# Attention and squared-ReLU feed-forward on one core: a last add in its own buffer, a later copy on GpSimd, and another rule for VectorE's hold-ups

## The chip, the cores and the metric

The kernel runs on one core of a Trainium2 chip. The metric is the device time of one execution in microseconds; before the change it is 402.41 us, the median of three runs (402.33 to 403.97). A core has TensorE (PE, matmuls; PEld, its weight loads), VectorE (DVE), ScalarE (ACT), GpSimd (POOL) and SyncE (SP), which only issues DMAs. Each engine executes its own queue in order, and engines wait for each other by semaphores.

## The reference

Eight sequences of 384 tokens go through grouped-query attention (16 query heads on 4 key and value heads, width 64), and the 1024 features of each token then through a feed-forward layer of width 2048 with a squared ReLU:

```python
scores = scale * np.matmul(q, k.transpose(0, 1, 3, 2))
scores = scores - np.max(scores, axis=-1, keepdims=True)
attn = np.exp(scores)
attn = attn / (np.sum(attn, axis=-1, keepdims=True) + 1e-09)
x = np.matmul(attn, v)              # then (8 * 384, 1024)
h = np.maximum(x @ w_in, 0.0)
out = h * h @ w_out                 # (3072, 1024), float32
```

## The kernel before, in words

**Batches and stages.** The work is done batch by batch (`b` from 0 to 7, one sequence each). A batch has scores (TensorE, L448), exponentials (ScalarE, L458), the product with the values (TensorE, L515 or L474) with its division (VectorE, L528 and L530), a transpose into `xT`, an up stage (`x @ w_in`), squares, and a down stage (`h*h @ w_out`). Attention of the next batches is interleaved with the feed-forward of the present one.

**Strassen's scheme.** From batch 2 on both products of the feed-forward are done with seven block products for eight, in float16. In the up stage (`strassen`, matmuls at L902) VectorE or ScalarE copies a product out of PSUM into `hr` (L878, L881), VectorE adds a later product to it (L886), ScalarE or GpSimd scales and clips it (L788, L791), and `close_squares` squares it into `h2T` on ScalarE, GpSimd or VectorE (L796, L800). In the down stage (`products`, `pair_of`, matmuls at L944) blocks of 128 tokens are taken in pairs: pair A holds the first two blocks of a batch; the third block of an even batch is kept in `h2x` (copied by GpSimd, L1199, in `sum_ops`) and makes pair D with the third of the next, odd batch. The left-hand sums of blocks are made by VectorE and GpSimd (L1180), those for the up stage by VectorE in `sums` (L658, the last of them L661); `summed` holds the batches for which the latter are recorded.

**A pair's results.** `done` in `pair_of` is called for each of the seven products. Products 1, 5 and 6 are copied from PSUM to a buffer `y_sb` with the scale `gs` (`copied`, L1094 on ScalarE, L1095 on VectorE); product 6 is copied twice, as `a2` and `b2`, if the two blocks have different scales. Products 2, 7, 3 and 4 are added to such a buffer by VectorE (`added`, L1101). After product 7 GpSimd adds its buffer `a3` to `p5` (L1133); product 4 is then added in place to `a3`. `put` sends a finished buffer to the output with a DMA of SP (L1308). In the last pair of the last batch product 3 comes last, as two whole pieces of 384 and 128 columns (L999), and the 128 columns of product 5 are added to `b2` ahead.

**Weights.** w_out is scaled and converted to float16 in 16 pieces (`here2`, L1226, on VectorE or ScalarE), and combined in `less2` (L1231) and `apart2` (L1238). These wait in the list `w2_q`. Ranges are measured by reductions whose result is spread over the partitions with a small cast (`top_of`, L675).

**A planner sets the order.** While the program is built, `Recorder.add` keeps a clock for each engine, with a cost in us given for each instruction, and the loops at the end (with `upkeep`) choose by these clocks which instruction comes next on which engine. `port=True` marks an instruction of VectorE that cannot run beside one of GpSimd; for it `Recorder.add` makes the cost longer by the overlap with GpSimd's last four instructions. A changed cost changes the clocks, and with them the order of all that is planned after it. In `upkeep` a piece of `w2_q` goes to VectorE if its clock is at most `lead` ahead of TensorE's, to ScalarE if that is true of its own. `Recorder.add` leaves out the wait for an earlier instruction of the same engine that only read what is now written.

The lines that choose the engine of a piece of w_out:

```python
lead = {"scalar": 0.6 if ff["b"] == 1 else 0.1, "vector": ... 0.9 if ff["b"] == 1 else 0.1}
able = [x for x in ("vector", "scalar") if eng in (x, "any") and R.clock[x] <= now + lead[x]]
```

Of the kernel before, what the change touches and what calls it, by code (L numbers as in the profile page):

```python
# [8 lines left out]
class Recorder:  # L9
# [36 lines left out]
    def add(self, eng, fn, reads=(), writes=(), dma=None, cost=0.1, issue=0.1, shared=(), after=(), port=False):  # L46
        i = len(self.ops)
        deps = self.deps_of(reads, writes)
        raw = {self.writer[r] for r in reads if r in self.writer}
        for r in reads:  # L50
            self.readers.setdefault(r, []).append(i)
        for w in writes:
            self.writer[w] = i
            self.readers[w] = []
        need = set(after)
        for d in deps:
            o = self.ops[d]
            if o["dma"] is None and o["eng"] == eng and dma is None:
                if eng in self.IN_ORDER or d not in raw:
                    continue  # L60
            need.add(d)
        if dma is not None:
            if dma in self.dma_last:
                need.add(self.dma_last[dma])
            self.dma_last[dma] = i
        start = max([self.clock[eng]] + [self.ops[d]["end"] for d in need])
        if dma is not None:
            self.clock[eng] = start + issue
            if eng == "gpsimd":
                self.pool.append((start, start + 0.3 * issue))  # L70
            q = eng
            begin = max(self.ring.get(q, 0.0), start + issue + 0.8)
            if shared and begin > start + issue + 0.8:
                shared = (3.0, shared[1])
            if shared and self.ring.get("gpsimd", 0.0) > begin:
                self.ring["gpsimd"] += shared[1]
                for o in self.ops:
                    if o["eng"] == "gpsimd" and o["dma"] is not None and o["end"] > begin:
                        o["end"] += max(0.0, min(shared[1], o["end"] - 1.2 - begin))
                cost = shared[0]  # L80
            self.ring[q] = begin + cost
            end = begin + cost + (1.5 if begin > 30 else 1.2 if eng == "gpsimd" else 0.7)
        else:
            if eng == "gpsimd":
                self.pool.append((start, start + cost))
            elif port:
                cost += 1.0 * sum(max(0.0, min(z, start + cost) - max(a, start)) for a, z in self.pool[-4:])
            self.clock[eng] = start + cost
            end = start + cost + (0.2 if eng == "tensor" else 0.07)
        self.ops.append(dict(eng=eng, fn=fn, dma=dma, need=need, signal=False, start=start, end=end))  # L90
        return i
# [57 lines left out]
def bass_gqa_attention__then__ffn_squared_relu_kernel(  # L149
# [619 lines left out]
    def close_squares(which):  # L769

        for x in [x for x in open_squares if which(x)]:
            open_squares.remove(x)
            i, r, dst, keys, relu, b = x
            assert b < FAST or b in ranged
            val = hr[r]
            two = val.rearrange("p (f t) -> p f t", f=2)
            end = R.ops[i]["end"]
            act, dve, pool = [max(R.clock[e], end) for e in ("scalar", "vector", "gpsimd")]
            slack = 1.5 * (b >= FAST and keys[0][1:] not in LAST_SQUARES)
            plans = [(act + 0.45 * (1 + relu) + slack, "ss"), (max(act + 0.52 * relu, pool) + 0.77 + 0.2, "sg")]  # L780
            if relu:
                plans.append((pool + 2.2 + 0.6, "gg"))
            elif not ff["now"]:
                plans.append((dve + 0.95 + 0.4, "sv"))
            one, other = min(plans)[1]
            to, by = small(b)
            if relu and one == "s":
                R.add("scalar", lambda e, val=val, to=to: e.activation(val, val, AF.Relu, scale=to),  # L788
                      reads=[("hr", r)] + by, writes=[("hr", r)], cost=0.54 if by else 0.45)
            elif relu:  # L790
                R.add("gpsimd", lambda e, val=val, to=to: e.tensor_scalar(val, val, to, 0.0, ALU.mult, ALU.max),  # L791
                      reads=[("hr", r)] + by, writes=[("hr", r)], cost=1.42)
            for _, c, t in keys:
                wrote[c, t] = b
            if other == "s":
                R.add("scalar", lambda e, dst=dst, two=two: e.activation(dst, two, AF.Square),  # L796
                      reads=[("hr", r)], writes=keys, cost=0.45)
            else:
                eng = dict(g="gpsimd", v="vector")[other]
                n = R.add(eng, lambda e, dst=dst, two=two: e.tensor_tensor(dst, two, two, ALU.mult),  # L800
                          reads=[("hr", r)], writes=keys, cost=0.77 if other == "g" else 0.95, port=other == "v")
                if other == "v":
                    hr_read[r] = (n,)

# [249 lines left out]
    def pair_of(b, pair, one, two):  # L1054
# [28 lines left out]

        ys = {}
        g1, g2 = b_1 % 3, b_2 % 3

        def slot(name):
            ys[name] = y_slot(b)
# [15 lines left out]
        def put(who, x, name, c0=0, c1=512):  # L1104
            bb, i3 = who
            send(bb, i3, 512 * x + c0, 512 * x + c1, ys[name], c0)

        def done(prod, at, *cols):
            flags.add(("done", b, pair, prod))
            if prod == 1:  # L1110
                copied(at, "a1", g1)
            elif prod == 2:
                added(at, g1, "a1", "a1")
                put(one, 0, "a1")
            elif prod == 5:
                copied(at, "p5", g2)
                ys["bank"] = at
            elif prod == 6:
                eng = copied(at, "a2", g2)
                if g1 != g2:  # L1120
                    copied(at, "b2", g1, eng)
                else:
                    ys["b2"] = ys["a2"]
                if b == B - 1 and pair == "D":
                    added(ys["bank"], g1, "b2", "b2", TAIL, 512, (R.writer[("y", ys["p5"])],))
            elif prod == 7:
                if g1 == g2:
                    slot("a3")
                else:
                    ys["a3"] = ys["a2"]  # L1130
                added(at, g2, "a2", "a3")
                y, z = ys["a3"], ys["p5"]
                R.add("gpsimd", lambda e: e.tensor_tensor(y_sb[z], y_sb[z], y_sb[y], ALU.add),  # L1133
                      reads=[("y", y), ("y", z)], writes=[("y", z)], cost=1.28)
                put(two, 1, "p5")
            elif prod == 3:
                added(at, g1, "b2", "b2", *cols)
                put(one, 1, "b2", *cols)
            else:
                added(at, g2, "a3", "a3")  # L1140
                put(two, 0, "a3")

        def product(prod, at):
            (a, na), (w, nw) = left(prod), right(prod)
# [4 lines left out]
    d_q = []  # L1149

    def sum_ops(b, double):
# [33 lines left out]
        def all_wrote(cs, ts=(0, 1)):  # L1185
            return all(wrote.get((c, t)) == b for c in cs for t in ts)
# [5 lines left out]
        if double:  # L1192
            for n, prod in ((0, 5), (1, 6), (3, None), (2, 3)):
                reads, go = op("D", n, None)
                d_q.append((lambda prod=prod: prod is None or ("done", b, "A", prod) in flags, reads, go, True))
        elif b < B - 1:
            keys = [("h2T", c, 1) for c in range(NFC)] + [("DS", b, "A", n, x) for n in (2, 3) for x in range(2)]
            d_q.append((lambda: all_wrote(range(NFC), (1,)), keys, lambda: R.add(
                "gpsimd", lambda e: e.tensor_copy(h2x[:, :, :], h2_16[:, :, 256:384]), reads=keys,  # L1199
                writes=[("h2x", b), ("h2x", b - 2)] + X_OVER, cost=2.0), True))  # L1200

# [325 lines left out]
    def below():  # L1527
        return not ff["tiles"] and not ff["now"]
# [95 lines left out]
    def upkeep(now):  # L1624
# [66 lines left out]
            add_sums(b)  # L1691
        while w2_q and w2_q[0][0]() and R.when(reads=w2_q[0][1], eng="none") <= now:
            eng = w2_q[0][3]
            lead = {"scalar": 0.6 if ff["b"] == 1 else 0.1, "vector": 0.5 if ff["b"] == FAST and not below() else -9 if m_q or lazy else 0.6 if below() else 0.9 if ff["b"] == 1 else 0.1}
            able = [x for x in ("vector", "scalar") if eng in (x, "any") and R.clock[x] <= now + lead[x]]
            if not able:
                break
            w2_q.pop(0)[2](*(able[:1] if eng == "any" else ()))
# [271 lines left out]
```

## Time and profile before

| | us |
|---|---|
| median of three runs | 402.41 |
| the profiled execution | 402.27 |
| its span, first to last instruction | 400.3 |
| TensorE busy | 389.6 |
| VectorE busy | 315.4 |
| ScalarE busy | 266.7 |
| GpSimd busy | 148.4 |

The granted clock of TensorE is 1.00 in nearly all of the span. All times are in us from the start of the span unless marked ns. A row of the order of work has the start, the length, engine, line, operation, the buffers written and read, shapes and a count; in brackets stand the idle time of the engine ahead of it and what ended that. A row of the waits has who waited, for whom, the total, how often and the longest. A row of a group has count, busy time and the mean in ns, and then idle time by what ended it. A row of a line's instructions has the shortest, median and longest in ns. Matmuls of 64 rows run in pairs on the two halves of the array, and their ends are modelled, so they overlap in the rows.

### The profile page before, as it was taken

To read this page: it belongs to the slowest core of one execution; us is meant where nothing else is said; L and a number is where in the kernel's file an instruction comes from. 1 tells how busy PE (TensorE), PEld (TensorE's weight loads), DVE (VectorE), ACT (ScalarE), POOL (GpSimd) and SP (SyncE) were. 2 spreads that over 40 slices of the span, in tenths; PEclk is the share of its full clock that TensorE was granted. 3 is DMA by queue.
4 is the path that set the end of the run, shared out by engine and by line. 5 is a ranking of instruction groups with operands and counts; after the bars stand their busy time and mean duration, and the time that the engine had idled before them with its cause. 6 is when DMAs were issued, how large, how long until landed. Compare 5 with 4: busy or idle time off the path is not lost.

```text
span 400.3 us, 15645 instructions
## 1 busy us (share of the span) xinstructions
PE 389.6 (97%) x7022; PEld 300.2 (75%) x7022; DVE 315.4 (79%) x652; ACT 266.7 (67%) x390; POOL 148.4 (37%) x169
## 2 busy tenths in 40 slices
PE   9999999999999999999999999998999999999995
PEld 6565764555666897588977999698987899789653
DVE  3689879899898987987987788986885688856644
ACT  6948999596655897768675587877783297426510
POOL 8665510245001664355332343444301144126111
PEclk9999999999999999999999999999999999999999
DMA  9999999995329873398597816697622223120022
GB/s 174 189 199 182 207 185 190 208 165 80 43 75 189 133 86 60 76 179 91 99 120 161 162 23 92 81 149 109 70 60 93 92 44 25 48 80 4 28 81 104
DMA packets 95634, 44.39 MB, mean 111 GB/s; under 512 B 75984, under 2 KB 89552, under 8 KB 95568
## 3 DMA queue, kind: packets, MB, share of 16 engines
q0 software_dynamic: 36672, 17.44, 35.6%
q1 hardware_dynamic: 58224, 25.47, 31.9%
q8 instruction: 55, 0.90, 1.0%
q10 hardware_dynamic: 672, 0.49, 0.4%
q14 instruction: 11, 0.09, 0.1%
HBM read 35.65 MB, written 12.58 MB: 121 GB/s over the span
## 4 chain that ended last, share of the span: by engine, by line
PE 78%; DVE 7%; DMA 7%; issue 4%; POOL 3%; ACT 1%; POOLq 0%; ACTq 0%; DVEq 0%
PE ps L944 27%; PE ps L902 26%; PE ps L515 6%; PE ps L448 6%; PE ps L611 6%; DMA w_in_sb<-in_moe_w_in_dram 5%; PE ps L1276 5%; DMA wx<-in_k_dram 1%; PE ps L474 1%; DVE w_out_sb L1226 1%; POOL w_in_sb L320 1%; DVE hr L624 1%; DVE y_sb L1101 1%; DVE w_out_sb L1238 1%; ACT h2T L796 1%
## 5 line engine op out<-in xcount | busy, mean ns | idle before, releaser
L458 ACT ACTIVATE expT<-ps 128x1024 bf16<-128x1024 f32 (+1 forms) x124 | 120.8, 1015 | 25.3 <-PE ps L448 25.2
L944 PE MATMUL ps<-w_out_sb,h2T 64*128 64x512 f16 x528 | 97.8, 376 | 0.5 <-DVE y_sb L1101 0.5
L902 PE MATMUL ps<-xT,w_in_sb 64*128 64x192 f16 x1152 | 84.8, 243 | 0.3 <-DVE y_sb L1101 0.3
L902 PEld LDWEIGHTS ps<-xT,w_in_sb 64*128 64x128 f16 x1152 | 71.2, 94 | 3.5 <-DVE y_sb L1101 0.5
L800 POOL TENSOR_TENSOR h2T<-hr 128x384 f16<-128x384 f32 x54 | 44.6, 845 | 51.7 <-ACT hr L788 51.6
L944 PE MATMUL ps<-area,xT 64*128 64x512 f16 x288 | 55.8, 376 | 0.0
L944 PEld LDWEIGHTS ps<-w_out_sb,h2T 64*128 64x128 f16 (+1 forms) x528 | 41.1, 94 | 15.8 <-DVE y_sb L1101 0.6
L448 PE MATMUL ps<-qT,kT 64*128 64x256 bf16 (+2 forms) x336 | 51.4, 326 | 0.6 <-ACT expT L458 0.4
L902 PE MATMUL ps<-s_all,wx 64*128 64x192 f16 x768 | 51.9, 242 | 0.0
L788 ACT ACTIVATE hr<-hr,bits 128x384 f32<-128x384 f32 x71 | 41.9, 609 | 11.8 <-DVE hr L886 11.5
L886 DVE TENSOR_TENSOR hr<-ps,hr 128x384 f32<-128x384 f32 x72 | 39.2, 555 | 9.4 <-PE ps L902 6.2
L902 PEld LDWEIGHTS ps<-s_all,wx 64*128 64x128 f16 x768 | 44.4, 94 | 0.9
L515 PE MATMUL ps<-v_aug,expT 64*128 64x65 bf16 x1680 | 43.7, 190 | 1.2 <-issue 0.6
L611 PE MATMUL ps<-xT,w_in_sb 64*128 64x384 bf16 x448 | 42.1, 323 | 1.0 <-DVE hr L624 0.6
L1101 DVE SCALAR_TENSOR_TENSOR y_sb<-ps,bits,y_sb 128x512 f32<-128x512 f32 (+2 forms) x38 | 26.9, 724 | 19.9 <-PE ps L944 13.3
L515 PEld LDWEIGHTS ps<-v_aug,expT 64*128 64x128 bf16 x1680 | 39.3, 94 | 2.7 <-DVE o_sb L530 0.7
L944 PE MATMUL ps<-area,h2T 64*128 64x512 f16 x144 | 36.4, 376 | 0.0
L1094 ACT ACTIVATE y_sb<-ps,bits 128x512 f32<-128x512 f32 x20 | 13.6, 687 | 33.7 <-PE ps L944 33.6
L878 ACT COPY hr<-ps 128x384 f32<-128x384 f32 x34 | 16.2, 479 | 27.2 <-PE ps L902 26.6
L611 PEld LDWEIGHTS ps<-xT,w_in_sb 64*128 64x128 bf16 x448 | 22.0, 94 | 16.2 <-DVE hr L624 1.8
L902 PE MATMUL ps<-s_all,w_in_sb 64*128 64x192 f16 x384 | 32.8, 243 | 1.3 <-issue 1.3
L902 PE MATMUL ps<-xT,wx 64*128 64x192 f16 x384 | 33.2, 243 | 0.7 <-issue 0.6
(147 smaller groups left out, 748.6 us busy)
## 6 DMA issues: line engine op xcount, KB each, us to landing
out_dram<-y_sb SPq DMA_DIRECT2D x45, 256.0 KB, 2.4
w_in_sb<-in_moe_w_in_dram POOLq DMA_DIRECT2D x8, 512.0 KB, 15.1
w_out_sb<-in_moe_w_out_dram POOLq DMA_DIRECT2D x4, 1024.0 KB, 28.9
q_st<-in_q_dram POOLq DMA_DIRECT2D x19, 192.0 KB, 5.2
q_st<-in_q_dram POOLq DMA_DIRECT2D x4, 384.0 KB, 23.1
k_st<-in_k_dram POOLq DMA_DIRECT2D x6, 192.0 KB, 4.1
k_st<-in_v_dram POOLq DMA_DIRECT2D x5, 192.0 KB, 5.0
wx<-in_q_dram POOLq DMA_DIRECT2D x2, 384.0 KB, 8.4
```

The costliest lines, as they stand in the source:

```text
L448: mm = pe.matmul(ps[:, base + x, m * wide:(m + 1) * wide], kT[at(b)][64 * x:64 * x + 64, u, :], q_cols(b, u // NJ, x, c0, c0 + wide))
L458: R.add("scalar", lambda e: e.activation(dst, src, AF.Exp, scale=0.125), reads=keys, writes=[("expT", slot(b, u), t) for u, _, _ in pieces ...
L515: m = pe.matmul(ps[:, p[x], n * DP:n * DP + D + 1], w, v_aug[b % 2][r, g * NJ + j, 0:D + 1], start=(n + j + y == 0), stop=(n + j + y == 2 ...
L611: m = pe.matmul(bank(4 + xs[x])[:, 0:S], w_in_sb[r, kc, c * 128:(c + 1) * 128], xT[b % NXT][r, kc, :], start=(phase < 2 and kc == 0), stop ...
L788: R.add("scalar", lambda e, val=val, to=to: e.activation(val, val, AF.Relu, scale=to), reads=[("hr", r)] + by, writes=[("hr", r)], cost=0. ...
L800: n = R.add(eng, lambda e, dst=dst, two=two: e.tensor_tensor(dst, two, two, ALU.mult), reads=[("hr", r)], writes=keys, cost=0.77 if other ...
L878: R.add("scalar", lambda e: e.copy(hr[r][:, :], src), reads=[("bank", at)], writes=[("hr", r)], cost=0.45, after=hr_read.pop(r, ()))
L886: R.add("vector", lambda e: e.tensor_tensor(hr[r][:, :], src, hr[r][:, :], ALU.add), reads=[("bank", at), ("hr", r)], writes=[("hr", r)], ...
L902: return lambda pe: pe.matmul(bank(at)[:, f * h:f * h + h], w[r, kc, c:c + 128], m[r, kc, :], start=(prod in (1, 5, 2) and y + f + kc == 0 ...
L944: return lambda pe: pe.matmul(bank(p.at)[:, 0:512], p.a(k, r), p.w(k, r), start=start, stop=stop, skip_group_check=True)
L1101: R.add("vector", lambda e: e.scalar_tensor_tensor(y_sb[z][:, c0:c1], bank(at)[:, c0:c1], gs[g], y_sb[y][:, c0:c1], ALU.mult, ALU.add), re ...
L1276: m = pe.matmul(bank(i)[:, 0:n], h2T[:, c, i3 * 128:(i3 + 1) * 128], w_out_sb[:, c, c0:c1], start=(c == 0), stop=(c == NFC - 1))
```

## The change

1. In `Recorder.add`, the extra cost of a marked instruction of VectorE is no longer the overlap with GpSimd's last four instructions, but the whole time until the end of one of the last six that has begun and not ended when it starts.
2. Squares on GpSimd or VectorE wait for those earlier readers of the same part of `h2T` that run on their own engine.
3. In the last pair of the last batch, the two copies of product 6 are put on ScalarE, and product 4 is added from `a3` into a buffer `a4` of its own.
4. GpSimd's copy into `h2x` is recorded only when the sums of the next batch are.
5. The lead of VectorE for pieces of w_out in batch 1 is 0.5 for 0.9.

```diff
@@ Recorder.add
-                cost += 1.0 * sum(max(0.0, min(z, start + cost) - max(a, start)) for a, z in self.pool[-4:])
+                cost += max([0.0] + [z - start for a, z in self.pool[-6:] if a <= start < z])
@@ close_squares
-                          reads=[("hr", r)], writes=keys, cost=0.77 if other == "g" else 0.95, port=other == "v")
+                          reads=[("hr", r)], writes=keys, cost=0.77 if other == "g" else 0.95, port=other == "v",
+                          after=tuple(d for key in keys for d in R.readers.get(key, ()) if R.ops[d]["eng"] == eng))
@@ pair_of
+        last = b == B - 1 and pair == "D"
...
-                eng = copied(at, "a2", g2)
+                eng = copied(at, "a2", g2, "scalar" if last else None)
                 if g1 != g2:
                     copied(at, "b2", g1, eng)
...
-                added(at, g2, "a3", "a3")
-                put(two, 0, "a3")
+                ys["a4"] = slot("a4") if last else ys["a3"]
+                added(at, g2, "a3", "a4")
+                put(two, 0, "a4")
@@ sum_ops
-            d_q.append((lambda: all_wrote(range(NFC), (1,)), keys, lambda: R.add(
+            d_q.append((lambda: b + 1 in summed and all_wrote(range(NFC), (1,)), keys, lambda: R.add(
@@ upkeep
-            lead = {..., "vector": ... else 0.9 if ff["b"] == 1 else 0.1}
+            lead = {..., "vector": ... else 0.5 if ff["b"] == 1 else 0.1}
```

More of the change, by code (lines that the diff above doesn't have):

```diff
@@ L1123, in done @@
                     ys["b2"] = ys["a2"]
-                if b == B - 1 and pair == "D":
+                if last:
                     added(ys["bank"], g1, "b2", "b2", TAIL, 512, (R.writer[("y", ys["p5"])],))
@@ L1693, in upkeep @@
             eng = w2_q[0][3]
-            lead = {"scalar": 0.6 if ff["b"] == 1 else 0.1, "vector": 0.5 if ff["b"] == FAST and not below() else -9 if m_q or lazy else 0.6 if below() else 0.9 if ff["b"] == 1 else 0.1}
+            lead = {"scalar": 0.6 if ff["b"] == 1 else 0.1, "vector": 0.5 if ff["b"] == FAST and not below() else -9 if m_q or lazy else 0.6 if below() else 0.5 if ff["b"] == 1 else 0.1}
             able = [x for x in ("vector", "scalar") if eng in (x, "any") and R.clock[x] <= now + lead[x]]
```

## The prediction

> **What bounds the kernel now.** I read the page's busy table first, then who waited for whom on TensorE, then the busy time by stage, and last the order of work around the places that the edits touch.
>
> The page's first part, the waits of TensorE, and busy time of three stages (stretch, its length, then PE, PEld, DVE, ACT and POOL busy with instruction counts, clock, DMA share, GB/s):
>
> ```profile
> PE 389.6 (97%) x7022; PEld 300.2 (75%) x7022; DVE 315.4 (79%) x652; ACT 266.7 (67%) x390; POOL 148.4 (37%) x169
> ...
> PE ps L902 <- issue: 2.0, 2, 1.3
> PE ps L611 <- DVE hr L624: 0.6, 2, 0.4
> PE ps L515 <- DVE o_sb L530: 0.5, 1, 0.5
> PE ps L944 <- DVE y_sb L1101: 0.5, 1, 0.5
> PE ps L902 <- DVE y_sb L1101: 0.3, 1, 0.3
> ...
> 79.30:97.70 18.40, 17.76 (x218) 10.17 (x216) 17.52 (x34) 16.54 (x21) 9.92 (x11) 1.00 0.90 150
> 137.00:141.00 4.00, 3.46 (x98) 2.84 (x94) 3.97 (x8) 2.41 (x5) 1.56 (x2) 1.00 0.73 98
> 396.00:400.30 4.30, 0.05 (x1) 0.00 (x0) 1.63 (x3) 0.00 (x0) 0.00 (x0) 0.87 0.51 183
> ```
>
> TensorE is the bound: 389.6 of 400.3 us. Of the 10.7 us that it is not busy, 4.25 lie behind its last matmul (last row), and the waits for VectorE sum to 0.6 + 0.5 + 0.5 + 0.3 = 1.9 us. So an edit of other engines can win in two places only: the 4.25 us tail, and those 1.9 us. The 2.0 us named issue are waits that the trace gives no cause for; no edit aims at them.
>
> **The tail: a buffer of its own, copies on ScalarE.** VectorE, then GpSimd, TensorE and SP at the end; then VectorE's forms from 391 us; then an earlier add beside GpSimd:
>
> ```profile
> 392.07 1.41 DVE L1095 TENSOR_SCALAR y_sb<-ps,bits 128x512 f32<-128x512 f32 x2 [2.70 <-PE ps L944]
> 393.52 1.03 DVE L1101 SCALAR_TENSOR_TENSOR y_sb<-ps,bits,y_sb 128x128 f32<-128x128 f32 x2
> 396.00 1.73 DVE L1101 SCALAR_TENSOR_TENSOR y_sb<-ps,bits,y_sb 128x512 f32<-128x512 f32 x3 [1.45 <-POOL y_sb L1133]
> ...
> 394.63 1.27 POOL L1133 TENSOR_TENSOR y_sb<-y_sb 128x512 f32<-128x512 f32 x1 [10.82 <-DVE y_sb L1101]
> ...
> 394.13 1.92 PE L999 MATMUL ps<-w_out_sb,xT 128*128 128x384 f16 x16
> ...
> 395.92 2.64 SPq L1308 DMA_DIRECT2D out_dram<-y_sb  x4
> 397.76 0.81 SPq L1308 DMA_DIRECT2D out_dram<-y_sb  x2
> ...
> L1101 DVE SCALAR_TENSOR_TENSOR y_sb<-ps,bits,y_sb 128x512 f32<-128x512 f32 x2 | 1.5, 751 | 1.4 <-POOL y_sb L1133 1.4
> L1101 DVE SCALAR_TENSOR_TENSOR y_sb<-ps,bits,y_sb 128x128 f32<-128x128 f32 x2 | 0.7, 350 | 0.1
> L1101 DVE SCALAR_TENSOR_TENSOR y_sb<-ps,bits,y_sb 128x384 f32<-128x384 f32 x1 | 0.6, 609 | 0.0
> ...
> 382.55 1.26 POOL L1133 TENSOR_TENSOR y_sb<-y_sb 128x512 f32<-128x512 f32 x1 [10.96 <-DVE y_sb L1101]
> 383.44 0.75 DVE L1101 SCALAR_TENSOR_TENSOR y_sb<-ps,bits,y_sb 128x512 f32<-128x512 f32 x1 [0.98 <-PE ps L944]
> ```
>
> VectorE stands idle for 1.45 us at 394.55: product 4's add writes the buffer that GpSimd is still reading. With its own buffer it starts at 394.55 and takes 0.75. Product 3 then sets the pace: its first part, 384 of 512 columns of the 1.92 us from 394.13, is ready near 395.6 and takes 0.61, its second when TensorE ends at 396.05, and takes 0.35. VectorE ends near 396.65 instead of 397.73, 1.08 us earlier. The add may run beside GpSimd at full speed: the one at 383.44 began inside GpSimd's 382.55 to 383.81 and took 0.75 all the same.
>
> The end is the last store, though. SP issues four, the last two 0.81 / 2 = 0.4 us apart, the first when GpSimd is done at 395.92, which does not move. The four then go at 395.92, 396.3, 396.7 and 397.05; the last one is now at 398.2. By issue the gain is 1.1 us. By bandwidth (stretches behind the end; then the last store's time to landing):
>
> ```profile
> 396.60:399.60 3.00, 0.00 (x0) 0.00 (x0) 1.03 (x3) 0.00 (x0) 0.00 (x0) 0.93 0.74 262
> 397.75:398.25 0.50, 0.00 (x0) 0.00 (x0) 0.00 (x0) 0.00 (x0) 0.00 (x0) 1.00 1.02 385
> 398.25:398.75 0.50, 0.00 (x0) 0.00 (x0) 0.00 (x0) 0.00 (x0) 0.00 (x0) 1.00 0.44 157
> ...
> out_dram<-y_sb SPq DMA_DIRECT2D x1, 64.0 KB, 1.7
> ```
>
> the four stores move 3.0 x 262 = 786 KB; at the best rate shown, 385 GB/s, that takes 2.04 us instead of 3.0, a gain of 0.9. I take 0.9, since both must hold, with 0 (the add waits after all) and 1.1 as ends. The two copies cost nothing either way: on VectorE the pair takes 1.41 us, and ScalarE is free; what they feed (the 128-column add, and behind it L999) starts within 0.1 us of where it did. If ScalarE were late, L999 would be, one for one.
>
> **GpSimd's copy behind the next sums.** The stretch where this copy hurts, GpSimd, VectorE, TensorE, then the range of the cast, and where the sums end:
>
> ```profile
> 252.91 1.90 POOL L1199 COPY area<-h2T 128x2048 f16<-128x2048 f16 x1
> 253.07 1.83 DVE L675 CAST top_w<-bits 128x128 bf16<-128x128 f32 x1
> 254.82 0.74 DVE L1101 SCALAR_TENSOR_TENSOR y_sb<-ps,bits,y_sb 128x512 f32<-128x512 f32 x1
> 255.62 0.39 PE L944 MATMUL ps<-w_out_sb,h2T 64*128 64x512 f16 x1 [0.46 <-DVE y_sb L1101]
> ...
> L675 DVE CAST top_w<-bits x14: 226/227/1829, 57.6 to 346.6; 128x128 bf16<-128x128 f32 x14
> ...
> 259.09 0.20 DVE L661 TENSOR_SCALAR bits<-bits 128x1 f32<-128x1 f32 x1
> 261.43 1.27 POOL L1133 TENSOR_TENSOR y_sb<-y_sb 128x512 f32<-128x512 f32 x1 [1.34 <-DVE y_sb L1101]
> ```
>
> A cast of 0.23 us became 1.83 and ended when the copy did; the add behind it came late, and TensorE lost 0.46 us. With the copy behind L661, at 259.1 to 261.0, the cast is back at 0.23 and these 0.46 us go. What the copy meets there is the pair's add at 261.43, 0.4 us after it; should one of GpSimd's loads go ahead of the copy, that add is late, and with it product 4's add, which writes what GpSimd reads there. What such a late add costs TensorE is shown by the wait of L902 for L1101, 0.3 us. The copy also moves behind the loads of queries that it held back, which can only be early by that. I take -0.45, between -0.46 and +0.3. The two other copies count as zero: TensorE's waits in the list are not at them.
>
> **Hold-ups in full, a shorter lead, a wait of squares for their own engine.** In batch 1 VectorE is full (17.52 of 18.40 us above) and converts w_out between evictions:
>
> ```profile
> 88.80 4.37 DVE L1226 TENSOR_SCALAR w_out_sb<-w_out_sb,bits 128x1024 f16<-128x1024 bf16 x6
> 93.08 1.00 DVE L624 TENSOR_SCALAR hr<-ps 128x384 f32<-128x384 f32 x2
> 94.15 0.82 PE L611 MATMUL ps<-xT,w_in_sb 64*128 64x384 bf16 x8 [0.19 <-DVE hr L624]
> ...
> L1226 DVE TENSOR_SCALAR w_out_sb<-w_out_sb,bits x14: 472/482/1680, 82.2 to 94.0; 128x1024 f16<-128x1024 bf16 x14
> L1226 ACT ACTIVATE w_out_sb<-w_out_sb,bits x2: 1147/1150/1152, 79.3 to 84.3; 128x1024 f16<-128x1024 bf16 x2
> ```
>
> Six in a row hold up the eviction of hr. A lead of 0.5 for 0.9 lets about one fewer (0.48 us) stand ahead of it, which covers the two waits for L624 (0.6 us in all). The formula itself moves both ways: it charges more where GpSimd is already running, nothing where GpSimd begins later. It changes the order from 73 us on, and I cannot derive that order by hand. I take -0.3 for both together, half of the 0.6, with ends of -1.9 (all waits for VectorE go) and the loss of the third rival.
>
> The squares' waits (rows of GpSimd's idle time):
>
> ```profile
> POOL h2T L800 <- ACT hr L788: 51.6, 25, 5.9
> POOL ident L1333 <- POOL ident L1332: 0.2, 1, 0.2
> ...
> L800 POOL TENSOR_TENSOR h2T<-hr x54: 816/826/1263, 133.3 to 366.9; 128x384 f16<-128x384 f32 x54
> ```
>
> a wait of GpSimd for itself showed 0.2 us; at 54 squares at most 11 us, against 51.6 us that the same squares wait for ScalarE. It counts as nothing; without that cover, what is queued behind a square on GpSimd, the sums of squares and the loads, would be late, and TensorE one for one. VectorE's few squares get the same wait, for sums that it finished a batch before.
>
> GpSimd's squares reach 1263 ns beside 826, so a hold-up runs the other way too, which neither formula charges to GpSimd; that 0.44 us lies in its idle time as well.
>
> **Sum.** 402.27 (this execution: span 400.3 and 2.0 around it; the median 402.41 is 0.14 above) - 0.9 - 0.45 - 0.3 = 400.6.
>
> **Rivals.** (1) The order settles better everywhere: all 1.9 us of waits for VectorE go (0.45 of them the copy's). 402.27 - 0.9 - 1.9 = 399.5; the hidden lateness at 137 to 141 us, where 0.54 us of TensorE are idle, makes 399.0. For it: the casts and conversions that were held up are just those that the new formula sees. Against: most such GpSimd work was queued after VectorE's op, which no formula sees.
> (2) Only the tail comes, and the new order elsewhere gives its gain back: 402.27 - 0.9 + 0.2 = 401.6. For it: any reorder of a queue that is 95% full makes some eviction late.
> (3) Slower: with the shorter lead, conversions go to ScalarE at 1.15 us each. It has 18.40 - 16.54 = 1.86 us free in that stage, so from the second moved one each delays the exponentials that free TensorE's banks. Six moved make 6.9 - 1.86 = 5.0 us, less 1.35 elsewhere: 405.9. From three on it eats the gain; from five on the kernel is slower by 0.5%. Against: ScalarE takes one only when it is at most 0.6 us behind TensorE.
> (4) The add and GpSimd shut each other out. In its own buffer the add starts at 394.55, just before GpSimd's 394.63; if GpSimd had to wait for it, GpSimd would begin at 395.3, and the four stores would go 0.67 us later than above, the last at 397.7 for 398.2. The tail gives 0.4: 402.27 - 0.4 - 0.75 = 401.1. If the add waited instead, it would give nothing: 401.5. Against: the add at 383.44, though there GpSimd had begun first.
> The Trainium skill (SBUF — State Buffer, section "Who interferes with whom") has a rule that bears on this: a VectorE instruction with two inputs in SBUF contends with a GpSimd instruction that reads SBUF, one with at most one does not, and whoever issues first keeps the shared ports for its whole length. This add reads PSUM, one buffer and one factor per partition; if the factor counts as an input, the rule gives this rival's 401.1, if not, the forecast, and the 0.75 us at 383.44 agrees with the latter as far as one order of starts can.
>
> **Chances.** 0.5% of 402.41 is 2.0 us, about what a measurement of this kernel can tell from no change; faster is below 400.4, slower above 404.4. Forecast 0.47, half of whose own range of 399.7 to 401.5 lies a little over the border (0.20 faster, 0.27 same). Rival 1: 0.20, faster. Rival 2: 0.17, same. Rival 3: 0.11 (0.09 slower, 0.02 same). Rival 4: 0.05, same. That makes 0.40, 0.51 and 0.09. The range 398.7 to 402.7 holds the forecast and rivals 1, 2 and 4.
>
> **What would show it.** Right: no idle VectorE between the adds at 394 us, its last add within 0.7 us of TensorE's last matmul; every L675 below 1.3 us in batch 4; fewer than six L1226 in a row. Wrong: more than three L1226 on ScalarE, new waits of TensorE for expT, or issue waits that grew: they would outweigh the rest without any edit having aimed at them.

## The result, and the profile after

The changed kernel takes 400.76 us, the median of 13 runs (399.2 to 401.99), against 402.33 us for the kernel before, measured beside it (13 runs, 401.19 to 403.97). The ratio is 0.9957, with a 95% interval of 0.9938 to 0.9976: between 1.0 and 2.5 us faster. The profiled execution took 401.29 us, its span 399.2 us.

The page's first part of the changed kernel, and TensorE's waits between 70 and 392 us (who, for whom, total, times, longest). The inserted lines move later line numbers by one to three: L902, L944, L999, L1101, L1133, L1199 and L1226 of before are L903, L945, L1000, L1103, L1135, L1202 and L1229 here.

```profile
PE 388.7 (97%) x7019; PEld 298.7 (75%) x7022; DVE 312.0 (78%) x648; ACT 270.0 (68%) x395; POOL 145.7 (36%) x168
...
PE ps L903 <- issue: 3.5, 2, 2.1
PE ps L611 <- DVE hr L624: 1.0, 2, 0.7
PE ps L515 <- ACT expT L458: 0.4, 1, 0.4
PE ps L903 <- DVE y_sb L1103: 0.3, 1, 0.3
PE ps L945 <- DVE y_sb L1103: 0.3, 1, 0.3
```

TensorE's waits for other engines are not fewer: 2.0 us here, 1.9 before. Two of them went (the add behind the held cast, and `o_sb` at 140 us), those in batch 1 grew from 0.6 to 1.0 us, and two are new: one of 0.4 us for ScalarE's `expT` at 148 us, and one of 0.3 us for VectorE's add at 211 us (L945). The waits named issue grew from 2.6 us (2.0 and 0.6) to 3.5.

The end, in the order of work of the changed kernel, VectorE, ScalarE, GpSimd, TensorE and SP:

```profile
393.27 2.02 DVE L1103 SCALAR_TENSOR_TENSOR y_sb<-ps,bits,y_sb 128x128 f32<-128x128 f32 x3 [4.00 <-ACT y_sb L1096]
393.70 1.59 DVE L1103 SCALAR_TENSOR_TENSOR y_sb<-ps,bits,y_sb 128x512 f32<-128x512 f32 x2
395.54 1.07 DVE L1103 SCALAR_TENSOR_TENSOR y_sb<-ps,bits,y_sb 128x384 f32<-128x384 f32 x2 [0.25 <-PE ps L1000]
...
391.97 1.26 ACT L1096 ACTIVATE y_sb<-ps,bits 128x512 f32<-128x512 f32 x2 [1.04 <-PE ps L945]
...
394.53 1.27 POOL L1135 TENSOR_TENSOR y_sb<-y_sb 128x512 f32<-128x512 f32 x1 [10.83 <-DVE y_sb L1103]
...
394.03 1.92 PE L1000 MATMUL ps<-w_out_sb,xT 128*128 128x384 f16 x16
...
395.32 2.15 SPq L1311 DMA_DIRECT2D out_dram<-y_sb  x4
```

VectorE no longer idles for GpSimd: product 4's add is the second of the two at 393.70 and ends at 395.29, while GpSimd works from 394.53 to 395.80. The last add ends at 396.61, 0.66 us behind the last matmul (395.95), and the first of the last four stores goes at 395.32, 0.5 us ahead of GpSimd's end, not after it. From the last matmul to the end of the span it is 3.25 us now, for 4.21 (the 4.25 of the prediction counts to the end of its stretch, 400.30; the span ends at 400.26).

The casts, GpSimd's copy, and the stretches of the copy, of batch 1, of 137 us and of the larger issue wait (stretch, length, busy time of PE, PEld, DVE, ACT, POOL, clock, DMA share, GB/s):

```profile
L675 DVE CAST top_w<-bits x14: 226/227/228, 56.8 to 346.5; 128x128 bf16<-128x128 f32 x14
...
259.30 1.90 POOL L1202 COPY area<-h2T 128x2048 f16<-128x2048 f16 x1
261.15 1.28 POOL L1135 TENSOR_TENSOR y_sb<-y_sb 128x512 f32<-128x512 f32 x1
...
250.00:264.00 14.00, 14.00 (x215) 11.76 (x212) 11.28 (x27) 11.32 (x13) 6.88 (x7) 1.00 0.67 85
79.30:97.70 18.40, 17.45 (x218) 9.94 (x216) 18.11 (x37) 15.76 (x20) 11.06 (x12) 1.00 0.93 157
137.00:141.00 4.00, 4.00 (x118) 3.74 (x112) 3.82 (x8) 3.54 (x6) 1.17 (x3) 1.00 0.28 53
179.60:181.60 2.00, 0.59 (x16) 0.43 (x14) 0.66 (x2) 1.93 (x3) 1.49 (x2) 1.00 0.18 34
```

No cast is held any more, TensorE is busy throughout the copy's stretch and at 137 us, but in batch 1 it has 17.45 us instead of 17.76, and near 181 us it stands for 1.4 us without a cause in the trace.

### The profile page after: what moved, and what is told of

Read it like the earlier page. It is cut to its first block, busy times and chain, and to the rows that moved or that the text cites. A ratio compares the mean times of both kernels' runs of the same rounds, so it can differ in the third digit from the quotient of the medians.

```text
span 399.2 us, 15638 instructions
## 1 busy us (share of the span) xinstructions
PE 388.7 (97%) x7019; PEld 298.7 (75%) x7022; DVE 312.0 (78%) x648; ACT 270.0 (68%) x395; POOL 145.7 (36%) x168
## 4 chain that ended last, share of the span: by engine, by line
PE 91%; DVE 4%; ACT 2%; issue 1%; DVEq 0%
PE ps L945 31%; PE ps L903 28%; PE ps L448 7%; PE ps L611 7%; PE ps L515 7%; PE ps L1279 5%; ACT expT L458 2%; PE ps L474 2%; PE ps L574 1%; DVE hr L624 1%; DVE w_out_sb L1229 1%; PE ps L1366 1%; DVE y_sb L1103 1%; PE ps L549 1%; PE ps L1000 0%
## 5 line engine op out<-in xcount | busy, mean ns | idle before, releaser
L945 PE MATMUL ps<-w_out_sb,h2T 64*128 64x512 f16 x528 | 98.0, 376 | 0.0
L903 PE MATMUL ps<-xT,w_in_sb 64*128 64x192 f16 x1152 | 84.1, 243 | 0.5 <-DVE y_sb L1103 0.3
L903 PEld LDWEIGHTS ps<-xT,w_in_sb 64*128 64x128 f16 x1152 | 70.9, 94 | 3.7 <-PE ps L903 0.5
L800 POOL TENSOR_TENSOR h2T<-hr 128x384 f16<-128x384 f32 x52 | 42.0, 828 | 50.1 <-ACT hr L788 50.0
L945 PE MATMUL ps<-area,xT 64*128 64x512 f16 x288 | 55.7, 376 | 0.0
L903 PE MATMUL ps<-s_all,wx 64*128 64x192 f16 x768 | 51.6, 243 | 0.0
L945 PEld LDWEIGHTS ps<-w_out_sb,h2T 64*128 64x128 f16 (+1 forms) x528 | 39.2, 94 | 16.4 <-ACT h2T L796 0.3
L1103 DVE SCALAR_TENSOR_TENSOR y_sb<-ps,bits,y_sb 128x512 f32<-128x512 f32 (+2 forms) x38 | 27.1, 725 | 23.2 <-PE ps L945 12.4
L903 PEld LDWEIGHTS ps<-s_all,wx 64*128 64x128 f16 x768 | 44.2, 94 | 0.9
L515 PE MATMUL ps<-v_aug,expT 64*128 64x65 bf16 x1680 | 43.1, 190 | 0.5 <-ACT expT L458 0.4
L515 PEld LDWEIGHTS ps<-v_aug,expT 64*128 64x128 bf16 x1680 | 39.2, 94 | 1.9 <-ACT expT L458 0.8
L945 PE MATMUL ps<-area,h2T 64*128 64x512 f16 x144 | 35.9, 376 | 0.0
L903 PE MATMUL ps<-s_all,w_in_sb 64*128 64x192 f16 x384 | 32.4, 242 | 2.1 <-issue 2.1
L903 PE MATMUL ps<-xT,wx 64*128 64x192 f16 x384 | 32.9, 242 | 1.4 <-issue 1.4
L1135 POOL TENSOR_TENSOR y_sb<-y_sb 128x512 f32<-128x512 f32 x9 | 11.9, 1319 | 61.1 <-DVE y_sb L1103 61.1
```

What stands on the lines that cost most here:

```text
L515: m = pe.matmul(ps[:, p[x], n * DP:n * DP + D + 1], w, v_aug[b % 2][r, g * NJ + j, 0:D + 1], start=(n + j + y == 0), stop=(n + j + y == 2 ...
L903: return lambda pe: pe.matmul(bank(at)[:, f * h:f * h + h], w[r, kc, c:c + 128], m[r, kc, :], start=(prod in (1, 5, 2) and y + f + kc == 0 ...
L945: return lambda pe: pe.matmul(bank(p.at)[:, 0:512], p.a(k, r), p.w(k, r), start=start, stop=stop, skip_group_check=True)
L1103: R.add("vector", lambda e: e.scalar_tensor_tensor(y_sb[z][:, c0:c1], bank(at)[:, c0:c1], gs[g], y_sb[y][:, c0:c1], ALU.mult, ALU.add), re ...
```

## The experiments

Single executions of one kernel lie up to 5.5 us apart (the kernel before, 25 runs in one comparison: 400.64 to 406.18), so beside the medians each trace was cut at places that every order has: the first matmul of batch 0's down stage (53 us), the first matmul of the up stages of batches 2 to 7, the last matmul, and the end of the span. All lengths are in us; the last two columns are the sums of TensorE's waits from 70 to 392 us, named issue (with those that the trace puts on TensorE's own scores) and for other engines.

| kernel | to up 2 | up 2 to 3 | 3 to 4 | 4 to 5 | 5 to 6 | 6 to 7 | 7 to last matmul | to the end | issue | others |
|---|---|---|---|---|---|---|---|---|---|---|
| before | 73.9 | 41.9 | 52.9 | 39.7 | 52.7 | 37.1 | 44.6 | 4.21 | 2.6 | 1.9 |
| before2 | 74.1 | 42.0 | 52.3 | 39.7 | 52.4 | 37.1 | 44.6 | 4.21 | 1.6 | 1.9 |
| tail | 73.8 | 41.9 | 52.5 | 39.7 | 52.7 | 37.1 | 44.6 | 3.23 | 2.0 | 1.9 |
| a4 | 73.6 | 41.9 | 52.3 | 39.7 | 53.0 | 37.1 | 44.6 | 3.24 | 2.1 | 1.9 |
| copy | 73.6 | 42.0 | 52.5 | 39.0 | 53.3 | 37.1 | 44.6 | 4.22 | 2.9 | 1.4 |
| lead | 73.5 | 42.4 | 52.4 | 39.8 | 52.5 | 37.1 | 44.6 | 4.20 | 1.2 | 3.1 |
| formula | 74.0 | 41.2 | 53.0 | 39.5 | 51.3 | 37.1 | 44.6 | 4.21 | 0.4 | 2.2 |
| formtail | 74.0 | 41.2 | 53.6 | 39.5 | 51.1 | 37.1 | 44.6 | 3.24 | 1.0 | 2.2 |
| formtailcopy | 74.1 | 40.6 | 53.7 | 39.0 | 52.0 | 37.1 | 44.6 | 3.25 | 1.7 | 1.8 |
| notail | 74.6 | 40.8 | 54.5 | 39.0 | 51.6 | 37.1 | 44.6 | 4.21 | 2.4 | 1.9 |
| after | 74.4 | 40.8 | 53.8 | 39.0 | 53.5 | 37.1 | 44.6 | 3.25 | 3.5 | 2.0 |
| after2 | 74.6 | 40.8 | 54.5 | 39.0 | 52.3 | 37.1 | 44.6 | 3.25 | 3.1 | 1.9 |
| fewturns | 74.4 | 40.8 | 54.5 | 39.0 | 51.5 | 37.1 | 44.6 | 3.24 | 2.3 | 1.9 |
| fewloads | 74.6 | 40.8 | 51.9 | 39.0 | 51.1 | 37.1 | 44.6 | 3.28 | 0 | 1.9 |

Most columns repeat within 0.1 us for one order of work; the first differs by up to 0.5 us (73.6 to 74.1 in before's order). The stages from up 3 to 4 and from up 5 to 6 differ more, by up to 1.9 us between executions of one order, and in them the issue waits lie.

**The tail alone, and everything but the tail.** On the kernel before, and taken back from the changed one:

```diff
+        last = b == B - 1 and pair == "D"
-                eng = copied(at, "a2", g2)
+                eng = copied(at, "a2", g2, "scalar" if last else None)
-                added(at, g2, "a3", "a3")
-                put(two, 0, "a3")
+                ys["a4"] = slot("a4") if last else ys["a3"]
+                added(at, g2, "a3", "a4")
+                put(two, 0, "a4")
```

> The kernel before with the third edit alone: product 4 of the last pair into a buffer of its own, product 6's two copies on ScalarE. The order of everything ahead of the last pair is unchanged. My theory: the whole gain of the end, 0.9 to 1.1 us against before, and the last matmul where it was (396.05 us in before's span, within what two executions differ); VectorE idles no longer for GpSimd between its last adds. Rival (the order elsewhere makes the gain): under 0.3 us.

> The changed kernel without the third edit. My theory: what is left is the copy on GpSimd (0.45 us) and the new order in batch 1 and 2 (between -0.5 and +0.5 us): 0 to 0.9 us faster than before, about 1 us slower than the changed kernel. At the end VectorE idles about 1.4 us for GpSimd again. Rival (the order makes the gain): 1.2 us or more faster than before.

The tail alone measured 401.93 us against 402.26 (ratio 0.9992, 0.9969 to 1.0014), too coarse to tell; in the trace the end is 0.98 us shorter and all else is as before, as my theory has it. The change without the tail measured 401.15 us against 402.26 (0.9971, 0.9954 to 0.9989): 1.1 us faster, 0.4 us slower than the changed kernel's median, while its trace ends 4.21 us behind the last matmul again. By the medians what is left is thus worth more than the 0 to 0.9 us that I expected, though the interval (0.4 to 1.9 us) reaches into that.

**Both kernels once more**, without an edit:

> The kernel before once more, for a second profile. TensorE's waits named issue, 2.0 us in the first profile: if they belong to the program, they come back at the same places (177 and 274 us) with the same lengths within 0.2 us; if they belong to the execution, they differ by 0.5 us or more, and explain why single executions of one kernel lie up to 2.8 us apart.

> The changed kernel once more, for a second profile. Its first profile has 3.5 us of waits named issue (181 and 274 us) against 2.0 before. If they belong to the execution, they differ here by 0.5 us or more; if they belong to the program's new order, they are 3.5 us again, and the new order costs 1.5 us that the edits gain elsewhere. In both cases the last matmul is 3.2 to 3.3 us ahead of the end of the span, against 4.25 before, and every cast L675 takes under 0.3 us.

These took 401.03 and 400.76 us. TensorE's issue waits of the two, by row; the first is before2:

```profile
PE ps L902 <- issue: 1.1, 1, 1.1
PE ps L515 <- issue: 0.5, 1, 0.5
```

```profile
PE ps L903 <- issue: 3.1, 3, 1.6
```

Both answers hold in part: the places belong to the order (the wait at 181 us is in every execution of the changed order but fewloads, below: 1.4 us in after, 1.5 to 1.6 us in after2, notail and fewturns), the lengths to the execution (that at 274 us is 2.1, 0.9 and 0.2 us in after, after2 and notail).

**The formula alone, the lead alone:**

```diff
-                cost += 1.0 * sum(max(0.0, min(z, start + cost) - max(a, start)) for a, z in self.pool[-4:])
+                cost += max([0.0] + [z - start for a, z in self.pool[-6:] if a <= start < z])
```

> The kernel before with the first edit alone, the hold-ups counted in full. The traces so far show TensorE's waits for other engines after 70 us: before 81.2, 93.9, 138.6, 139.9 and 254.4 us (1.9 us in all); with all edits 82.4, 93.5 and 147.5 (1.7 us). Theory A: the formula makes the new order. Then the waits near 138 and 140 are gone, one of 0.5 near 147 is there, and those of batch 1 are 1.1 to 1.2 us, while that at 254 (the copy) stays. Theory B: the lead makes it; then the waits are those of before. Time: within 1 us of before in either case.

```diff
-            lead = {..., "vector": ... else 0.9 if ff["b"] == 1 else 0.1}
+            lead = {..., "vector": ... else 0.5 if ff["b"] == 1 else 0.1}
```

> The kernel before with the fifth edit alone, the lead of 0.5 for 0.9 in batch 1. Theory A (the formula makes the order): the waits of batch 1 change by less than 0.2 us, those at 138 and 140 stay. Theory B (the lead makes it): the two near 138 and 140 are gone and one near 147 is there. Third possibility: the lead alone, under the old formula, moves conversions to ScalarE and TensorE waits for expT by more than 0.5 us; then it costs 1 us or more.

The formula alone gives 400.07 us against 401.9 (0.9959, 0.9944 to 0.9974), more than any other edit and outside the 1 us that I had allowed; the lead alone 401.3 against 401.9 (0.9994, 0.9976 to 1.0012), nothing that can be told. The wait at 140 us (0.5 us) goes under each of the two; the one near 148 us and the longer ones in batch 1 come only when both are there. So neither theory of a single author holds. TensorE's waits with the formula alone:

```profile
PE ps L944 <- DVE y_sb L1101: 1.1, 3, 0.5
PE ps L611 <- DVE hr L624: 0.6, 2, 0.5
PE ps L902 <- issue: 0.4, 1, 0.4
PE ps L902 <- DVE y_sb L1101: 0.3, 1, 0.3
PE ps L515 <- DVE o_sb L530: 0.2, 1, 0.2
```

The waits for other engines are 2.2 us, more than before; what is gone is issue, 0.4 for 1.6 to 2.9 us in the five executions with before's order in those stages. In the table the gain is 0.7 us from up 2 to 3 and 1.1 to 2.0 us from up 5 to 6, less 0.1 to 0.8 us lost from up 3 to 4. What the formula changed from up 5 to 6 can be seen in the traces: GpSimd issues its load of values (L302) 7.8 us into that stage in `formula` and `formtail`, which have no issue wait there, and 5.7 us into it in all other kernels; of these, the ten that keep loads and transposes whole wait 0.2 to 2.1 us there. With the lead alone, conversions on ScalarE rose from two to four:

```profile
L1226 ACT ACTIVATE w_out_sb<-w_out_sb,bits x4: 1139/1145/1151, 80.9 to 92.4; 128x1024 f16<-128x1024 bf16 x4
```

and TensorE's waits for other engines to 3.1 us, most of them for VectorE from 129 us on, none of note for expT.

**The copy alone:**

```diff
-            d_q.append((lambda: all_wrote(range(NFC), (1,)), keys, lambda: R.add(
+            d_q.append((lambda: b + 1 in summed and all_wrote(range(NFC), (1,)), keys, lambda: R.add(
+                          after=tuple(d for key in keys for d in R.readers.get(key, ()) if R.ops[d]["eng"] == eng))
```

> The kernel before with the second and fourth edits, GpSimd's copy behind the next sums and the squares' wait. All three casts L675 that were held (0.82, 1.21 and 1.83 us) take: the one at 253 0.23, that at 163 0.23, that at 169 still over 1 us if GpSimd's add holds it. TensorE's wait of 0.39 us near 254 is gone, its other waits stay as before; last matmul 0.4 us earlier but for what single executions differ.

One execution, 401.27 us. The second edit, the squares' wait, has no run of its own: it is in this kernel and in all that have the copy, and no trace of them lists a wait of a square for GpSimd itself. No cast is above 228 ns, also not the one near 169 us that I thought GpSimd's add would go on holding; the stage from up 4 to 5 is 0.7 us shorter, and the copy's stretch is full (taken 2 us earlier, as this execution runs ahead of the changed kernel's there):

```profile
248.00:262.00 14.00, 14.00 (x202) 11.98 (x200) 10.82 (x25) 11.62 (x14) 6.87 (x7) 1.00 0.68 91
```

**The buffer without the copies on ScalarE:**

```diff
+                ys["a4"] = slot("a4") if last else ys["a3"]
+                added(at, g2, "a3", "a4")
```

> The kernel before with half of the third edit: product 4 of the last pair into a buffer of its own, the copies where they were. With both halves the span's end came 3.23 to 3.25 us behind the last matmul, before 4.21. Theory: the buffer does it all, 3.2 to 3.3 us here; the two copies on ScalarE are worth 0.05 us or less, and L999 waits 0.2 us as ever. Rival: the copies free VectorE for product 7's add, and without them 3.5 us or more remain.

401.07 us in one execution, and 3.24 us from the last matmul to the end: the buffer does it all.

**Combinations**: the formula and the tail; and with the copy, which is the changed kernel without the shorter lead (0.9 again):

> The kernel before with the first and third edits, the formula and the tail; the order ahead of the last pair is that of the formula alone. Theory: the two gains add, since the tail's is behind the last matmul: 1.8 + 1.0 = 2.8 us below before, 399.3 at a before of 402.1; end of the span 3.2 to 3.3 us behind the last matmul, waits named issue under 1 us as with the formula alone. Rival: the formula's 1.8 us were a lucky sample; then 1.0 to 1.6 us below before, and issue waits of 2 us or more.

> The changed kernel without the fifth edit, the shorter lead. Theory A: the lead is what gives the formula's gain back; then this is 3 us or more below before, and TensorE's issue waits are under 1 us. Theory B: the later copy on GpSimd, by moving loads and transposes, brings the issue waits back; then they are 2 us or more here, and the time is that of the changed kernel within 0.8 us.

The first gave 399.58 us against 402.35 (0.9931, 0.9907 to 0.9955), 2.8 us less as the theory had it; the second 399.6 (0.9933, 0.9899 to 0.9966), also 2.8 us less. For the second neither theory holds as it was put: the gain is a little under 3 us, and the issue waits are 1.7 us, between the two. Their rows of issue waits, formtail first (the trace puts the wait at 181 to 182 us in both on TensorE's own scores):

```profile
PE ps L902 <- PE ps L448: 1.0, 1, 1.0
```

```profile
PE ps L903 <- PE ps L448: 1.0, 1, 1.0
...
PE ps L903 <- issue: 0.7, 1, 0.7
```

By the medians both beat the changed kernel by 1.2 us, though the intervals overlap; what the table adds is that the shorter lead, on top of the formula, costs 0.3 to 0.6 us up to up 2, in every one of five executions, and, but for fewloads (below), sits with longer issue waits, 2.3 to 3.5 against 1.7. The copy, 0.5 us from up 4 to 5 and 0.6 from up 2 to 3, is not seen in the median beside the formula: what it wins there the stage from up 5 to 6 had against it in that execution. There GpSimd's load is back at 5.7 us into the stage, and a wait of 0.7 us with it, which is what theory B had in mind, at a third of its size.

**What the issue waits are for.** Two kernels of the same order as the changed one; from batch 4 on, the first makes the DMA transposes smaller, the second the loads:

```diff
-            out=kT[at(b)][:, 6 * half:6 * half + 6, :], in_=k_dup[:, 6 * half:6 * half + 6]...
+            out=kT[at(b)][:, 6 * half:6 * half + (6 if b < 4 else 1), :], in_=k_dup[:, 6 * half:6 * half + (6 if b < 4 else 1)]...
-            out=qT[at(b)][:, 12 * half:12 * half + 12, :], in_=q_st[at(b)][:, 8 * half:8 * half + 8, :]...
+            out=qT[at(b)][:, 12 * half:12 * half + (12 if b < 4 else 3), :], in_=q_st[at(b)][:, 8 * half:8 * half + (8 if b < 4 else 2), :]...
```

> The changed kernel with the DMA transposes of keys and queries from batch 4 on cut to a sixth and a quarter of their size (as many DMAs, waits and instructions, the same order; the scores of those batches are computed from what older batches left there). The waits named issue at 181 and 274 us are 3.1 to 3.5 us in the changed kernel. Theory: TensorE's instruction blocks come late behind these transposes; then both waits together fall under 1 us, and the time by 2 us or more. Rival: the loads are what they come late behind, or the program's own place of the blocks; then they stay over 2 us.

```diff
-            q_st[st][:, h0:h1, :], q[b, h0:h1]...
+            q_st[st][:, h0:h1 if b < 4 else h0 + 1, :], q[b, h0:h1 if b < 4 else h0 + 1]...
+            # keys and values: [:, 0:HKV if b < 4 else 1] on both sides
```

> The changed kernel with the loads of queries, keys and values from batch 4 on cut to a quarter or less (as many DMAs and waits, the same order; the rest of those tensors is what older batches left there). Theory (the transposes delay the instruction blocks): the waits named issue stay over 2 us. Rival: the loads delay them; then both fall under 1 us, and the time by 2 us or more.

With small transposes the kernel takes 400.56 us (0.9938 of before, 0.9909 to 0.9966), and the issue waits are 2.3 us. With small loads it takes 397.74 us against 402.35 (0.9882, 0.9844 to 0.9919), 3.0 us below the changed kernel's median, and no issue wait is left:

```profile
PE ps L611 <- DVE hr L624: 0.9, 2, 0.7
PE ps L515 <- ACT expT L458: 0.4, 1, 0.4
PE ps L903 <- DVE y_sb L1103: 0.3, 1, 0.3
PE ps L945 <- DVE y_sb L1103: 0.3, 1, 0.3
...
179.60:181.60 2.00, 2.00 (x62) 1.89 (x58) 1.72 (x4) 1.93 (x4) 0.63 (x1) 1.00 0.15 31
```

My theory of the transposes fell for the wait at 181 us, which is 1.6 us with small transposes and gone with small loads. The one at 274 us is gone in both, in single executions of a wait that was 0.2 to 2.1 us before, so there the transposes are not ruled out. What passes through the queues shortly before TensorE stands still in the changed kernel (147 packets that began between 178.7 and 178.9 us, by queue: packets, MB, share of the 16 engines):

```profile
q0 software_dynamic: 55, 0.02, 83.2%
q1 hardware_dynamic: 91, 0.02, 51.3%
q8 instruction: 1, 0.02, 38.5%
```

A block of 16 KB of instructions (0.02 MB in the row) began at 178.73 us among the loads' packets (the software queue) and landed at 179.96. TensorE stopped at 179.92 and went on at 181.33, 1.4 us behind the landing (start, length and what, in the order of time):

```profile
179.68 0.25 PE ps L903 x6
179.92 1.41 issue
```

The other traces show that this is what it waited for. There are 27 such waits between 70 and 392 us in the fourteen of them, the two put on the scores included. Each ends 1.3 to 1.7 us after a block of 16 KB has landed. They lie at four places only of TensorE's stream of matmuls and weight loads, near the 5535th, the 5790th, the 6045th and the 9610th, the first three 256 instructions apart; and in no trace does TensorE pass one of these places sooner than 1.2 us after the landing. With small loads the block for the 5790th began when TensorE was some 210 instructions away from it, in the changed kernel some 65; the block itself took no longer (1.23 us there, 1.45 us with small loads). So TensorE waits for its own instructions, and the loads make the block begin late. That the shorter lead does this by bunching the loads is likely, not shown: GpSimd issues the last three loads of queries ahead of that wait within 1.5 us in the five executions with both edits, within 3.7 us in `formula`, `formtail` and `formtailcopy`.

## Why the prediction was right or wrong

**The total** was right: 400.6 us predicted, 400.76 measured, faster by 0.4%. That it came so close is in part luck: the tail and the copy came as predicted or better, but the third term, -0.3 us, stands for effects that were neither seen ahead nor small.

**The tail** was right in size, 0.9 predicted, 0.96 to 0.98 in the traces. VectorE's last add ended 0.66 us behind the last matmul, where 0.60 was worked out. Two details were not right: the new buffer's store went ahead of GpSimd's instead of behind it, and the stores' rate (786 KB at 385 GB/s) set the end less than their issue did. The DMA engines were full, with shares of 1.00 to 1.03 from 396.2 to 398.2 us, but the last store landed 1.77 us behind its issue for 1.71 before, so the full engines cost it some 0.06 us, and its issue came 1.02 us earlier against the last matmul. The two estimates lay too close for it to matter. Zero for ScalarE's copies was right. Rival 4 is out: add and GpSimd began within 0.02 us of each other and kept 0.75 and 1.27 us. The Trainium skill (SBUF — State Buffer, "Who interferes with whom") says that a VectorE instruction with at most one input in SBUF does not contend with GpSimd; this trace agrees if the factor per partition does not count as an input.

**The copy** was right in its mechanism: the held cast went, and with it the wait of 0.46 us at 255 us. With the squares' wait beside it, it was sized too low: 0.7 us from up 4 to 5 for the 0.45 predicted, and where zero was put for the copy of batch 2, the stage from up 2 to 3 gained 0.6 us once the formula was there (41.2 to 40.6) and nothing without it.

**The formula and the lead** came out near -0.3 for the wrong reasons, and this is the step that failed: "A lead of 0.5 for 0.9 lets about one fewer stand ahead of it, which covers the two waits for L624 (0.6 us in all)". These waits rose to 0.9 to 1.0 us in all five executions that have both edits. The larger of the two, 0.45 us at 81.41, never stood behind a conversion: in the kernel before, VectorE's first one starts at 82.19, and what held up the eviction was mostly a reduction of 0.93 us (L673). With all edits the same reduction stands ahead of it and comes later. Before, then after:

```profile
79.22 0.93 DVE L673 TENSOR_REDUCE bits<-area 128x1 f32<-128x768 bf16 x1
80.33 1.95 DVE L624 TENSOR_SCALAR hr<-ps 128x384 f32<-128x384 f32 x4
82.19 1.21 DVE L1226 TENSOR_SCALAR w_out_sb<-w_out_sb,bits 128x1024 f16<-128x1024 bf16 x2
...
80.46 0.93 DVE L673 TENSOR_REDUCE bits<-area 128x1 f32<-128x768 bf16 x1
81.57 1.02 DVE L624 TENSOR_SCALAR hr<-ps 128x384 f32<-128x384 f32 x2
82.65 1.15 PE L611 MATMUL ps<-xT,w_in_sb 64*128 64x384 bf16 x12 [0.69 <-DVE hr L624]
```

So at most the other wait, 0.2 us, was within the lead's reach. A second step failed with it: "So an edit of other engines can win in two places only". The waits named issue (2.6 us in that trace; the prediction left out the 0.6 us of L515) were a third place, and the largest: the formula, which I took to move both ways, gave 1.8 us alone, most of it from up 5 to 6, where GpSimd's load comes 2 us later and no issue wait is left. The shorter lead, by the medians, gave a part of that back. I had said that issue waits could outweigh the rest without an edit aiming at them; they did, in the formula's favour and then, as far as the medians tell, against the lead.

**The signs.** Those named for right all came: VectorE no longer idles for GpSimd between the adds, its last add is 0.66 us behind the last matmul, no L675 is above 0.23 us, and at most five conversions stand in a row. But two of the three named for wrong came as well: a new wait for expT (0.4 us) and issue waits that grew from 2.6 to 3.5 us.

**Rivals 1 and 2**: waits for VectorE did not vanish (1.6 us for 1.9), so rival 1 did not happen; rival 2's picture, gains here and losses there, is what the waits for other engines show. **Rival 3** needed three conversions more on ScalarE; there was one (three for two), and the waits for expT that it should have brought in batch 1 did not come; the one of 0.4 us at 148 us is outside that stage.

**Left open.** Taken from the traces alone, with the five executions of before's order (before, before2, tail, a4, copy) and three of the changed one (after, after2, notail), each left out where its own edits differ, the stages that repeat give -0.96 (end), -0.7 (up 4 to 5), -1.2 (up 2 to 3) and +0.75 (to up 2), together -2.1 us; the two stages with issue waits were 1.75 us longer and 0.4 us shorter on the mean, +1.35. That is -0.75 us against -1.6 measured, short of the interval (1.0 to 2.5 us); the stretch ahead of the first cut, which differs by 1.1 us among these eight, is not in it, and a few profiled executions are too little to say more. What the shorter lead costs is open too: the ratios with and without it are 0.9957 and 0.9933, and their intervals overlap.

## What to carry to other kernels

Where a planner written into the program orders the work, any change of a cost moves transfers too, and their effect on the instruction stream can be larger than the wait that was aimed at: cut the trace at places that every order has, and compare stage by stage before believing a median. A value tuned under one cost formula (the lead) should be tried again after the formula changes, in both settings; here the old value was the better one by the medians, though the intervals overlap. An in-place add at the end of a kernel is worth a buffer of its own if another engine still reads the old one.

## What the runs showed of the hardware

TensorE stood for 0.2 to 2.1 us at a time with no instruction of another engine behind it, at four places of its instruction stream, until 1.3 to 1.7 us after a 16 KB block of instructions had landed. Cutting the loads of queries, keys and values from batch 4 on to a quarter or less took these waits away (3.5 and 3.1 us to none); cutting the transposes left 2.3 us. A cast of 0.23 us that began inside a copy of GpSimd took 1.83 us and ended within 0.1 us of it. A VectorE add with one buffer in SBUF beside PSUM ran at its 0.75 us beside a GpSimd add that had begun before it or at the same time.
